# A spectral filter and a gated feed-forward block: the first batch in another order, and its weight rounding spread out

## The chip, the core and the metric

The kernel runs on one core of a Trainium2 chip. The metric is the device time of one execution in microseconds (us); lower is better. The kernel before takes 3011.8 us (median of three runs, 3008.76 to 3013.31).

The core has five engines that work side by side, each on its own list of instructions in order: TensorE (PE, with its weight loads listed apart as PEld), VectorE (DVE), ScalarE (ACT), GpSimd (POOL) and SyncE (SP), which here only issues transfers (DMA). They wait for each other with semaphores. Matmul results appear in PSUM, everything else is in SBUF; DRAM is reached by DMA.

## The reference

```python
# x: (8, 3008, 256) float32; filt_r, filt_i: (1505, 256)
X = np.fft.rfft(x, axis=1)
Y = X * (filt_r + 1j * filt_i)[None]
x = np.fft.irfft(Y, n=3008, axis=1).astype(np.float32).reshape(24064, 256)

g   = x @ w_gate                      # w_gate, w_val: (256, 1536), float64
val = x @ w_val
out = (g / (1 + np.exp(-g)) * val) @ w_out     # w_out: (1536, 256), float64
```

Eight batches of 3008 tokens go through a filter along the sequence, and each token then through a gated feed-forward block. The weights come in double precision; the kernel itself rounds them to single precision.

## The kernel before

**The filter.** A length of 3008 is 47 x 64. Stage 1 multiplies with a 47-point table, its result (D1) goes through DRAM (in the first batch it stays in SBUF and is turned with TensorE); stage 2 does the 64-point transform (`stage2a`), multiplies with the filter, and goes back (`stage2b`) in 12 pieces of two residues each; its result (D2) goes to DRAM; stage 3 multiplies with the inverse 47-point table and leaves y, one chunk of 752 tokens at a time. There are four chunks in a batch.

**The feed-forward block.** A chunk is worked on three times, once for each third ("group") of the 1536 hidden units, so a batch has 12 steps (chunk k, group g). Within a step a fast form of the matrix product needs combinations of weights and of tokens: P and Q products take y itself, A, B and E products take sums of two blocks of y (in `y_t`, made by `combine_sequence`) and combinations of weights (made by `combine_weights`). All 26 weight pairs of a group make 3.4 MB, which is kept in DRAM once made, and reloaded in four pieces for each step. The order within a step is a fixed list of tokens; W are the products with `w_out`, o their additions, S the sums of h, x.o the output stores, t the places where pieces of the filter of the following chunk or batch go:

```python
SCHEDULE = """
Q0 o3' t4.2' W2 f0 S00' S01' x0.o' t0.0 x1.o' Q1 t0.1 x2.o' P3 x3.o' f1 t4.3' W1 x4.o' S10' x03 S11'
s13 x5.o' P1 o1 t0.2 P0 o2 c1 D01 A13 g1 c0 ...            # a mark (') means: for the step before
"""
```

The function `pin` keeps each instruction where the program puts it.

**Rounding the weights.** There are 36 half blocks of 256 KB. One is rounded so (cut):

```python
def round_half(i):
    raw, (use, *at) = raws[i], weights[i][1]
    low, high = raw[:, :, :, 0], raw[:, :, :, 1]
    pw = rpool.tile(..., tag="pw", bufs=2)
    w = rpool.tile(..., tag="w", bufs=2)
    pin(v.tensor_scalar(out=man, in0=high, scalar1=0xFFFFF, op0=ALU.bitwise_and))         # L282
    pin(v.tensor_scalar(out=pw, in0=high, ... logical_shift_right, bitwise_and))           # L284
    pin(nc.scalar.activation(out=w, in_=man, func=AF.Copy, scale=2.0 ** -20, bias=1.0))    # L286
    pin(nc.scalar.activation(out=pf, in_=pw, func=AF.Relu, bias=off_t))                    # L288
    pin(nc.scalar.activation(out=pf, in_=pf, func=AF.Relu, bias=top_t, scale=-1.0))        # L289
    pin(nc.scalar.activation(out=pw, in_=pf, func=AF.Copy, scale=-(2.0 ** 23), ...))       # L290
    load_weights(i + NRAW - 1)
    yield
    pin(v.scalar_tensor_tensor(out=pw, in0=raw high, 0x80000000 ... and, or))              # L295
    pin(v.scalar_tensor_tensor(out=w, in0=raw low, scalar=2.0 ** -52, in1=w, mult, add))   # L298
    # then one to five products and sums on GpSimd, into wt_t, wt_1 or wo_t

def round_next():            # called at a token: starts one half and ends the one before
    ...
```

Some calls stand between the stages of the start, the others at fixed tokens of the first three steps:

```python
PREPARE = {(0, "B03"): [("k", 1, p) for p in range(4)], ...}     # "k": keep a group's weights in DRAM
for step, tokens in ((0, "Q0 P3 P0 Q2 A01 B01"), (1, "Q0 P3 P1 A13 P2 B13 Q3 A12 B02 B12"),
                     (2, "A13 P2 B01 A02")): ...                  # "r": round one half
```

**The start.** The order in which the first batch is read, and its stage 2:

```python
for i, n in enumerate((0, 2, 2, 4)):
    spec.load_x(i)                               # a quarter of x
    for _ in range(n):
        load_weights(len(raws))                  # a half block of weights
for i in range(3):
    spec.load_tables(i)                          # tables and filters of 4 of the 12 pieces
...
lag = 3
for u in range(N_TWO + lag):
    if u < N_TWO:
        spec.turn(u + 2); run(spec.stage2a(u)); spec.real_part(u + 3)
    if u >= lag:
        run(spec.stage2b(u - lag))               # ends with ACT's copy and the store of D2

def stage2a(self, u):                            # (cut)
    pin(v.tensor_tensor(out=pt, in0=ps, in1=fr, op=ALU.mult))     # fr: filter's real part on both
    pin(v.scalar_tensor_tensor(out=qt[lo], in0=ps[hi], ...))      # halves, copied by ACT (real_part)
    pin(v.tensor_tensor(out=qt[hi], in0=ps[lo], in1=fi, op=ALU.mult))
    pin(add(nc.gpsimd, pt, pt, qt))
```

Of the kernel before, what the change touches and what calls it, by code (L numbers as in the profile page):

```python
# [51 lines left out]
NJ = NM // 2  # L52
# [6 lines left out]
NH = 4  # L59
# [3 lines left out]
TOK = (0, 128, TH - 128)  # L63
NG = 3
# [35 lines left out]
PAIRS = ((0, 1), (1, 2), (2, 3), (0, 2), (1, 3), (0, 3))  # L100
ORDER = [t for t in SCHEDULE if t[0] in "PQABE"]
# [41 lines left out]
def kernel(  # L143
# [22 lines left out]
    xpool = pool("xp", 3)  # L166
# [24 lines left out]
    def weights_of(b, k, g):  # L191
        return wt_1 if (b, k, g) == (0, 0, 1) else wt_t

    dram_tiles = [wdpool.tile([2 * NS, N2, C], FP32, name=f"d{1 + i % 2}_{i // 2}")
                  for i in range(4)]
    w_dram = wdpool.tile([NG, 128, NPR, 2, 128], FP32, name="w_all")
# [34 lines left out]
    def weight_halves():  # L231
# [16 lines left out]
        for g in range(NG):  # L248
            for i in BLOCKS:
                yield from hid(g, i)  # L250
            for j in range(JB * (g - 1), JB * g) if g else ():
                yield from proj(j)
        for j in range(JB * (NG - 1), NJ):
            yield from proj(j)
# [3 lines left out]
    NRAW = 3  # L258
    N_EARLY = 16

    def load_weights(i):
# [6 lines left out]
        queue = nc.sync if i < 9 else nc.scalar  # L268
        pin(queue.dma_start(out=raws[i], in_=weights[i][0]))

    def round_half(i):
# [4 lines left out]
        pw = rpool.tile([128, 2, 128], U32, name=f"pw_{i}", tag="pw", bufs=2)  # L276
# [6 lines left out]
                            op0=ALU.bitwise_and))  # L283
        pin(v.tensor_scalar(out=pw, in0=high, scalar1=20, scalar2=0x7FF,  # L284
                            op0=ALU.logical_shift_right, op1=ALU.bitwise_and))
        pin(nc.scalar.activation(out=w, in_=man, func=AF.Copy, scale=2.0 ** -20, bias=1.0))  # L286
        pf = pw.bitcast(FP32)
        pin(nc.scalar.activation(out=pf, in_=pw, func=AF.Relu, bias=off_t))  # L288
        pin(nc.scalar.activation(out=pf, in_=pf, func=AF.Relu, bias=top_t, scale=-1.0))  # L289
        pin(nc.scalar.activation(out=pw, in_=pf, func=AF.Copy, scale=-(2.0 ** 23),  # L290
                                 bias=255 * 2.0 ** 23))

        load_weights(i + NRAW - 1)
# [3 lines left out]
                                   op0=ALU.bitwise_and, op1=ALU.bitwise_or))  # L297
        pin(v.scalar_tensor_tensor(out=w.rearrange(flat), in0=raw.rearrange(flat2)[:, :, 0],  # L298
                                   scalar=2.0 ** -52, in1=w.rearrange(flat),
                                   op0=ALU.mult, op1=ALU.add))  # L300
        e = nc.gpsimd
# [23 lines left out]
    halves = [round_half(i) for i in range(len(weights))]  # L325
    rounding = [0]

    def round_next():

        i = rounding[0]  # L330
        rounding[0] += 1
        for h in halves[i:i + 1] + (halves[i - 1:i] if i else []):
            next(h, None)

    def combine_weights(g, i, j):
# [5 lines left out]
        if d == 1:  # L341
            pin(negated_sum(m, ui, uj))
        else:
            pin(add(nc.vector, m, ui, uj))
            pin(nc.vector.tensor_scalar(out=m, in0=m, scalar1=-1.0 / d, scalar2=None, op0=ALU.mult))
# [8 lines left out]
    def reload_weights(g, piece):  # L354
        a, b = PIECES[piece]
        tc.keep_in_program_order(nc.sync.dma_start(out=wt_t[:, a:b], in_=w_dram[g, :, a:b]))

    PREPARE = {(0, "B03"): [("k", 1, p) for p in range(4)], (1, "B03"): [("k", 2, 0)],  # L360
               (2, "A01"): [("k", 2, p) for p in (1, 2, 3)]}
    for step, tokens in ((0, "Q0 P3 P0 Q2 A01 B01"), (1, "Q0 P3 P1 A13 P2 B13 Q3 A12 B02 B12"),
                         (2, "A13 P2 B01 A02")):
        for token in tokens.split():
            PREPARE.setdefault((step, token), []).append("r")
    for g, pairs in ((1, "0Q313 0A0201 0A1202 0B0212 0B1223 0A2303"),
                     (2, "1A0213 1E1201 1E0202 2Q112 2P123 2Q203")):
        for p in pairs.split():
            PREPARE.setdefault((int(p[0]), p[1:-2]), []).insert(0, ("c", g, int(p[-2]), int(p[-1])))
# [21 lines left out]
    class Spectral:  # L391
# [50 lines left out]
        def load_tables(self, i):  # L442

            n = NS // 3
# [6 lines left out]
        def load_t4(self, k, i):  # L451
            self.t4[k, i] = t4pool.tile([NK, NH, C], FP32, name=f"t4_{self.b}_{k}_{i}", tag="t4")
            self.load(out=self.t4[k, i], in_=self.d2_rows[:, ts(2 * k + i, NH), :])
# [486 lines left out]
```

## Time and profile before

| what | value |
|---|---|
| span of the profiled execution | 3008.6 us |
| TensorE, busy | 2930.9 us, 97% of the span |
| weight loads of TensorE, busy | 2836.1 us, 94% |
| VectorE, ScalarE, GpSimd, busy | 64%, 54%, 52% |
| data moved | 545.5 MB, 181 GB/s in the mean |

The profile is of one execution. Its page gives busy times of the engines, the span in 40 slices of 75 us (a digit is the busy share in tenths), the chain of work that ended last, and groups of equal instructions with their mean duration and with the idle time of the engine just before them and what ended it. In lines such as `wa<-y_t,wt_t` the output stands left, the inputs right; L626 is a line of the kernel (626 the products of a step, 703 the W products, 641 the ScalarE copy "f" that negates a first product, 219, 222 and 226 helpers for sums and differences, 548 stage 3, 505 stage 2a, 532 stage 2b). A timeline line gives the start, the duration, engine, line, operation and count of merged instructions, and in brackets the idle time before and what ended it. Matmuls are in float32[...], so one product of the program is several matmul instructions.

### The profile page before, as it was taken

How to read it: one execution, taken by the hardware profiler on the slowest of the kernel's cores; microseconds unless marked ns; L12 is line 12 of the kernel's file. 1: busy time of each engine (PE TensorE's matmuls, PEld its weight loads, DVE VectorE, ACT ScalarE, POOL GpSimd, SP SyncE). 2: the span in 40 equal slices, each digit the busy share in tenths (PEclk: the TensorE clock that was granted, in tenths of full speed). 3: DMA queues.
4: the chain of work that ended last, by engine and by line, in shares of the span. 5: the costliest groups of instructions: out<-in, count | busy, mean ns of one | idle time of the engine just before them, and what ended most of it. 6: DMA issues, size and time to landing. Idle time of an engine off the chain costs nothing.

```text
span 3008.6 us, 57532 instructions
## 1 busy us (share of the span) xinstructions
PE 2930.9 (97%) x20286; PEld 2836.1 (94%) x20286; DVE 1920.6 (64%) x4385; ACT 1627.2 (54%) x4206; POOL 1578.4 (52%) x1763
## 2 busy tenths in 40 slices
PE   7589999999999999999999999999999999999999
PEld 5479999999999999999999999999999999999999
DVE  5675676566765666557665576655676566766665
ACT  6565555555555555555555545555545555555554
POOL 3664645455645455546554556544655445654453
PEclk8789999999999999999999999999999999999999
DMA  8445665556655656456655575556664556544442
GB/s 218 138 169 184 214 199 165 185 186 194 212 165 179 207 188 213 150 186 207 198 174 184 173 227 184 182 171 194 197 215 156 188 186 202 193 161 145 139 135 90
DMA packets 203849, 545.53 MB, mean 181 GB/s; under 512 B 28992, under 2 KB 99760, under 8 KB 202704
## 3 DMA queue, kind: packets, MB, share of 16 engines
q1 hardware_dynamic: 153002, 466.50, 48.6%
q10 hardware_dynamic: 41632, 51.46, 5.2%
q0 software_dynamic: 8928, 23.89, 2.6%
q8 instruction: 163, 2.67, 0.4%
q14 instruction: 124, 1.02, 0.1%
HBM read 459.68 MB, written 82.05 MB: 180 GB/s over the span
## 4 chain that ended last, share of the span: by engine, by line
PE 92%; DVE 0%; ACT 0%; issue 0%; POOL 0%; ACTq 0%
PE wa L626 24%; PE wA L703 17%; PE wk L626 16%; PE we L626 12%; PE wG L703 8%; PE wF L703 4%; PE pd L548 3%; PE pa L465 3%; PE pb L505 2%; PE pc L532 2%; DVE o L219 0%; DVE pw L284 0%; DVE y L226 0%; DVE h L222 0%; DVE h L219 0%
## 5 line engine op out<-in xcount | busy, mean ns | idle before, releaser
L626 PE MATMUL wa<-y_t,wt_t 128*128 128x188 f32 x4560 | 900.1, 323 | 5.8 <-ACT m L661 2.7
L626 PEld LDWEIGHTS wa<-y_t,wt_t 128*128 128x128 f32 x4560 | 747.0, 190 | 31.2 <-issue 15.2
L626 PE MATMUL wk<-y,wt_t 128*128 128x188 f32 x3040 | 583.0, 325 | 34.2 <-ACT f L641 24.0
L219 POOL TENSOR_TENSOR h<-h 128x376 f32<-128x376 f32 x190 | 182.7, 984 | 815.9 <-DVE h L673 815.9
L703 PE MATMUL wA<-wo_t,h 128*128 128x128 f32 x4608 | 579.8, 276 | 3.7 <-DVE o L219 2.7
L703 PEld LDWEIGHTS wA<-wo_t,h 128*128 128x128 f32 x4608 | 565.1, 192 | 16.9 <-issue 12.0
L222 POOL TENSOR_TENSOR h<-h 128x376 f32<-128x376 f32 x570 | 553.0, 994 | 0.5
L626 PEld LDWEIGHTS wk<-y,wt_t 128*128 128x128 f32 x3040 | 491.9, 191 | 63.8 <-ACT f L641 25.4
L222 DVE TENSOR_TENSOR we<-we,m 128x376 f32<-128x376 f32 x576 | 319.0, 556 | 202.4 <-PE we L626 145.5
L626 PE MATMUL we<-y_t,wt_t 128*128 128x188 f32 x2280 | 440.5, 323 | 0.0
L626 PEld LDWEIGHTS we<-y_t,wt_t 128*128 128x128 f32 x2280 | 377.5, 190 | 0.1
L222 POOL TENSOR_TENSOR D<-f,f 128x376 f32<-128x376 f32 x288 | 280.2, 986 | 110.0 <-ACT f L641 109.3
L226 DVE SCALAR_TENSOR_TENSOR y<-wk,c 128x376 f32<-128x376 f32 x480 | 244.5, 543 | 141.0 <-ACT we L657 87.0
L661 ACT COPY m<-wa 128x376 f32<-128x376 f32 x576 | 272.2, 473 | 89.9 <-PE wa L626 88.8
L668 ACT ACTIVATE g<-wa 128x188 f32<-128x188 f32 x576 | 188.3, 327 | 196.1 <-PE wa L626 188.4
L703 PE MATMUL wG<-wo_t,h 128*128 128x128 f32 x2304 | 289.5, 276 | 0.6 <-DVE o L219 0.6
L703 PEld LDWEIGHTS wG<-wo_t,h 128*128 128x128 f32 x2304 | 282.7, 192 | 0.8 <-DVE o L219 0.8
L668 ACT ACTIVATE u<-we 128x188 f32<-128x188 f32 x576 | 189.3, 329 | 168.2 <-DVE we L222 149.2
L641 ACT ACTIVATE f<-wk 128x376 f32<-128x376 f32 x288 | 139.7, 485 | 242.2 <-PE wk L626 223.3
L645 ACT COPY c<-wk 128x376 f32<-128x376 f32 x288 | 136.1, 473 | 227.4 <-PE wk L626 227.2
L648 DVE SCALAR_TENSOR_TENSOR x<-wk,f 128x376 f32<-128x376 f32 x192 | 104.4, 544 | 236.8 <-PE wk L626 236.2
L657 ACT COPY we<-y 128x376 f32<-128x376 f32 x480 | 223.6, 487 | 31.3 <-DVE h L673 12.9
(128 smaller groups left out, 3856.3 us busy)
## 6 DMA issues: line engine op xcount, KB each, us to landing
wt_t<-w_all SPq DMA_DIRECT2D x186, 896.0 KB
wt_t<-w_all SPq DMA_DIRECT2D x186, 768.0 KB
t<-d SPq DMA_DIRECT2D x64, 384.0 KB
d<-t ACTq DMA_DIRECT2D x112, 192.0 KB
lent<-de_tbl SPq DMA_DIRECT2D x84, 256.0 KB
lent<-in_filt_r_dram SPq DMA_DIRECT2D x336, 64.0 KB
lent<-d SPq DMA_DIRECT2D x84, 256.0 KB
d<-lent ACTq DMA_DIRECT2D x84, 256.0 KB
```

Source lines behind the costliest of these rows:

```text
L219: return eng.tensor_tensor(out=dst, in0=a, in1=b, op=ALU.add)
L222: return eng.tensor_tensor(out=dst, in0=a, in1=b, op=ALU.subtract)
L226: return nc.vector.scalar_tensor_tensor(out=dst, in0=a, scalar=-1.0, in1=b, op0=ALU.mult, op1=ALU.subtract)
L465: pin(nc.tensor.matmul(out=ps[0:NK], lhsT=wf_t, rhs=self.x.pop(u), start=True, stop=True))
L626: pin(nc.tensor.matmul(out=ps[:, z], lhsT=self.wt[:, SLOT[p], z], rhs=rhs, start=start and z == 0, stop=True, skip_group_check=True))
L641: pin(act.mul(self.small(f"f{i}", f"f{i}", 1), t[f"k{i}"], -1.0))
L645: pin(act.copy(out=self.small(f"c{i}", f"c{i}", 1), in_=t[f"k{i}"]))
L648: pin(v.scalar_tensor_tensor(out=dst, in0=t[f"k{j}"], scalar=-1.0, in1=t[f"f{i}" if j == 3 else f"D{at}"], op0=ALU.mult, op1=ALU.add))
L657: pin(act.copy(out=self.bank(f"e{at}"), in_=t[f"y{at}"]))
L661: pin(act.copy(out=self.small(f"m{at}", "m", 4), in_=t[f"a{at}"]))
L668: pin(act.activation(out=self.small(op, "g", 3, 1)[:, 0], in_=ps[:, 1], func=AF.Silu))
L703: pin(nc.tensor.matmul(out=self.tiles[at][:, t, :], lhsT=self.hs[i][:, HID[p], t0:t0 + 128], rhs=wo_t[:, JB * q + i, WO[p], :], start=star ...
```

## The change

It concerns the first batch. Its steps ran (0,0) (0,1) (0,2) (1,0) and so on, in pairs of chunk and group, so all three groups' weights were needed within the first three steps. Now the first three chunks take turns: (0,0) (1,0) (2,0) (0,1) (1,1) (2,1) (0,2) (1,2) (2,2), then chunk 3. Group 1 is needed from step 3 on and group 2 from step 6, and weights are not reloaded until then. For this, y, its sums and the partial outputs of a chunk are kept in DRAM between its turns. The rounding of one half is cut into five pieces, of which one is issued at each of 24 evenly spaced places of a step. At the start, tables come in sixths, and in another order with x and weights; the copy of the filter's real part is left out for every third piece (which multiplies its two halves separately). D2 for chunk 0 is read in two row ranges into a table buffer. In all batches the input has two buffers instead of three, and the outputs two instead of one.

```diff
+NT = 3
+PAIRS_USED = ((1, 3), (0, 1), (0, 2), (1, 2), (2, 3), (0, 3))
-    xpool = pool("xp", 3)
+    xpool = pool("xp", 2)
-        return wt_1 if (b, k, g) == (0, 0, 1) else wt_t
+        return wt_1 if b == 0 and k < NT and g == 1 else wt_t
-    NRAW = 3
-    N_EARLY = 16
+    NRAW = 2
+    N_EARLY = 15
     ... round_half: pw in 3 buffers, and a yield after each of five pieces (cut)
-            pin(nc.vector.tensor_scalar(out=m, in0=m, scalar1=-1.0 / d, scalar2=None, op0=ALU.mult))
+            pin(nc.scalar.mul(m, m, -1.0 / d))
     ... PREPARE is replaced by (cut)
+    class Preparation:
+        def tick(self, step, n=1):
+            for _ in range(n):
+                if self.window and self.window[0] <= step:
+                    self.window = next(self.steps, None)
+        def finish(self, step): ...
+    TICKS = 24
     ... load_tables
-            n = NS // 3
+            n = NS // 6
     ... the start
-        for i, n in enumerate((0, 2, 2, 4)): ...
+        load = [("x", 0), ("x", 1), ("w", 0), ("x", 2), ("w", 1), ("x", 3), ("t", 0), ("w", 2),
+                ("t", 1), ("w", 3), ("t", 2), ("w", 4), ("w", 5), ("t", 3), ("w", 6), ("t", 4),
+                ("w", 7), ("t", 5)]
     ... after stage 1 of the first batch
+        for i in range(8, N_EARLY):
+            load_weights(i)
     ... in the loop over the 12 pieces
+                preparation.tick(0, 1 + u % 2)
+                spec.real_part(u + 1)
+                preparation.tick(0)
     ... before stage 3
+        preparation.tick(0, 14)
     ... the order of steps, what is kept and reloaded
+        if b == 0:
+            steps[:NT * NG] = [(k, g) for g in range(NG) for k in range(NT)]
+    for step in range(NT):
+        for d, token in ((2, "Q2"), (1, "A01"), (3, "Q3")):
+            chore(step, token, keep_sums, step, d)
+        chore(step, "Q2" if step == 0 else "W2", keep_y, step)
+    for step in range(NT - 1, NT * NG):
+        chore(step, "A02", lambda s: reload_y(order_of(0)[s + 1][0], s), step)
+    for step in range(NT, NT * NG):
+        chore(step, "Q3", lambda s: new_outs(0, *order_of(0)[s]), step)
     ... stage 3 of chunk k + 1 is done within step k, four pieces and one of stage 1 (before: over
     ... two steps or later), and in the list of tokens
+                if b == 0 and this and place * TICKS % len(SCHEDULE) < TICKS:
+                    preparation.tick(step)
-                if op in ends and not last and (b or step > 1):
+                if op in ends and not last and (b or step >= NT * NG - 1):
                     reload_weights((g + 1) % NG, ends[op])
```

## The prediction

> **What bounds the kernel now.** I read the page from the top: busy time in 40 slices first, because a share over the whole span hides a bad stretch. Then came the waits of TensorE, longest first, then the same engines in windows of 25 us, and last the timeline of TensorE from 80 to 260 us, to find where each step (a chunk with one group of blocks) begins. The busy rows of the page (one digit for each 75 us):
>
> ```profile
> PE   7589999999999999999999999999999999999999
> PEld 5479999999999999999999999999999999999999
> ...
> PEclk8789999999999999999999999999999999999999
> ```
>
> From the fourth slice on TensorE is full, its weight loads too, and its clock is granted in full. Only the first 225 us have anything to give. The waits of TensorE over the whole span (engine, line, what it waited for; total, times, longest) say the same, since all of them lie there:
>
> ```profile
> PE wk L626 <- ACT f L641: 28.8, 5, 19.8
> PE wpb L505 <- ACT room L495: 11.5, 1, 11.5
> PE wk L626 <- DVE y L219: 10.2, 1, 10.2
> PE wa L626 <- ACT m L661: 3.4, 2, 2.7
> ```
>
> The three largest wait for ScalarE or VectorE, none for a transfer. Windows of 25 us (busy us of PE, PEld, DVE, ACT, POOL, then granted clock, DMA share, GB/s):
>
> ```profile
> 0.00:25.00 25.00, 20.89 (x127) 17.02 (x128) 7.45 (x17) 10.09 (x16) 1.53 (x7) 0.95 0.95 247
> ...
> 100.00:125.00 25.00, 5.17 (x14) 3.76 (x14) 14.09 (x31) 14.41 (x33) 15.90 (x26) 0.57 0.28 80
> ...
> 300.00:325.00 25.00, 25.00 (x180) 24.69 (x179) 18.92 (x42) 12.19 (x32) 15.46 (x16) 1.00 0.70 222
> ```
>
> At 100 to 125 us the busiest engine, GpSimd, has work for 15.9 of 25 us, and DMA for a quarter. That is a chain of small dependent operations, not a full engine. Three lines of TensorE's timeline mark the beginnings of steps 0, 1 and 3; the second line shows the long wait inside step 0:
>
> ```profile
> 100.23 1.62 PE L626 MATMUL wk<-y,wt_t 128*128 128x188 f32 x4 [10.23 <-DVE y L219]
> ...
> 125.23 2.88 PE L626 MATMUL wk<-y,wt_t 128*128 128x188 f32 x8 [19.84 <-ACT f L641]
> ...
> 154.06 0.80 PE L626 MATMUL wk<-y,lent 128*128 128x188 f32 x4
> ...
> 240.61 0.80 PE L626 MATMUL wk<-y,wt_t 128*128 128x188 f32 x4
> ```
>
> Step 2 begins at 202.6 in the same list. So steps 0, 1, 2 take 53.8, 48.6 and 38.0 us; later ones take 29.9 us (the last "wk" of step 3 is at 255.6, of step 12 at 524.7: 269.2/9). From 240.6 to the end at 3008.6, **2768.0 us** are TensorE's own work, which the change leaves alone.
>
> What fills the first stretch is rounding the double-precision weights: 36 halves, each 4 operations on VectorE, 4 on ScalarE, then 1 to 5 on GpSimd. The groups of instructions between 100 and 230 us give their means:
>
> ```profile
> L284 DVE TENSOR_SCALAR pw<-raw 128x256 uint32<-128x256 uint32 x20 | 11.7, 585 | 0.0
> ...
> L282 DVE TENSOR_SCALAR w<-raw 128x256 uint32<-128x256 uint32 x20 | 11.1, 556 | 8.1 <-POOL lent L219 3.2 <-POOL wo_t L305 2.4 <-POOL wt_t L219 1.5
> ...
> L286 ACT ACTIVATE w<-w 128x256 f32<-128x256 uint32 x23 | 9.6, 417 | 23.0 <-DVE w L282 22.6 <-DVE w L298 0.4
> ```
>
> ScalarE waited 22.6 us for VectorE's first operation of a half, and that one waited for GpSimd to give back the buffer of two halves before. A half is recorded as one lump, so the three engines pass it round in about 3 us (L282 starts at 110.43, 113.43, 116.43 us), and the step's own work queues behind it.
>
> **What the Trainium skill says.** "Perfetto Trace Analysis", Optimization Strategy: where the most-contended engine changes over time, interleaving those regimes may help. That is what the change does, and the windows above show the two regimes. "SBUF — State Buffer", SBUF: two separate sides: VectorE in a two-port mode and GpSimd take a shared port pair as an exclusive lock, the loser blocks. The trace agrees as far as durations go: the L284 operations on the raw halves take 0.280 us at the least and 1.073 at the most for one shape. "TensorE: Matmul & The Clock Gate", What's actually happening: an idle window halves the clock. It was granted 0.50 from 110 to 125 us, and a "wk" product meanwhile averages 393 ns against 323 later. "DMA: Bandwidth & Descriptors", Queues, rings and completion order: descriptors of a ring are consumed in order; I use this below for writes queued behind loads, and no run has shown that yet.
>
> **The change part by part.**
>
> *Start, up to the first product (100.2 us before).* Ahead of the first tables stood four x loads and eight weight halves (5.2 MB) and a third of the tables (2.1 MB); now it is x (3.1 MB), two halves (0.5) and a sixth (1.05), 4.65 MB. At the 247 GB/s of the first window that is 19 us, some 21 with the landing. Stage 2 can start at about 24 us; its first matmul now starts at 35.6, and then stands from 38 to 50 behind four lumps of rounding (the 11.5 us wait). VectorE paces stage 2: three operations of 0.69 us for each of 12 pieces, 2.16 us each. The change leaves out ScalarE's copy of the filter for every third piece, which then has four operations: 8 x 3 + 4 x 4 = 40 at 0.71 is 28.4 us. Six halves are rounded in between (24 operations of 0.27 to 0.42 in VectorE's timeline before 50 us, 8.3 us): 37 us, so 24 + 37 = 61 against 75.5 for the last such operation before. One new wait works against it: seven more halves (1.8 MB) are loaded by SyncE's queue ahead of the first store of D2. 11.5 + 1.8 + 0.26 MB at 247 GB/s land at 55 us, and with four buffers the ScalarE copy of piece 4, due near 48, waits for it. I take 4 us of the 7 as lost: 65. From there to stage 3 took 10.8 us before (75.5 to 86.3) and its steps are the same: 76. Then y took 13.9 us with rounding in front; without most of it, 4 to 5. **First product at 80.**
>
> *Step 0.* Before, six halves stood in lumps in it and four more right ahead of it. Now 24 pieces of rounding (five make a half, so 4.8 halves) are spread over the tokens. TensorE's floor is low, as there is nothing yet to project: 29.9 less 84 matmuls of 0.112 (1.34 for 12) is 20.5. But stage 3 of the next chunk is now wholly in this step, sums on GpSimd come 5 us before the first A product, and chains are short of slack: **28 us**, to 108.
>
> *Steps 1 and 2.* They now need the same third of the weights as step 0, so no rounding is due before step 3. In step 1, GpSimd has 8 h sums and 3 differences at 0.99 (10.9 us), the next chunk's sums (three operations each of 128x376, 128x564 and 128x188, which take 0.99, 1.38 and 0.59 between 600 and 1320 us: 8.9) and 4.8 halves of some three operations at 0.46 (6.6): 26.4 of 29.9. VectorE has 19 of steady work (64% of 29.9) and 19 rounding operations at 0.51 (9.7): 28.8. Both fit, with little to spare, and each in fixed order: **33 us each**, to 174. Before, step 3 began at 240.6: 66.6 us less.
>
> *Steps 3 to 8.* They keep rounding (to step 6) and save and reload y, its sums and the outputs: in step 3 some 3.4 MB of weights stored, 2.5 of y and sums, 1.6 of outputs, 1.0 of x, 1.3 of halves, 1 of D1, near 11 MB in 30 us. 360 GB/s is above the 231 that the 25 us windows reach from 225 to 600 us (398 was seen in 5 us with weight stores). Weight reloads (20 MB) fall away in steps 2 to 7. I charge **6 us** for all six steps. Two input buffers instead of three in the other batches: x is issued about 12 us before its use instead of 18; I charge nothing.
>
> Sum: 80 + 28 + 33 + 33 + 6 + 2768 = 2948 span, and 3 for the measured median being above the profiled span (3011.8 and 3008.6): **2951 us**, a ratio of 0.980.
>
> **The rivals.** (1) *VectorE or GpSimd becomes the bound of steps 1 to 5*, as they come to 28.8 and 26.4 of 29.9 us. For it: the lock, and 4 halves with 6 combinations in step 2 before cost 8 us over 29.9. Against: those were lumps. It would make these steps 36 and the time about 2970. (2) *Reloads arrive late*: the next chunk's sums (1.7 MB in three loads) must land before its A products, behind stores in the same queue. The transfers total near the limit in steps 3 and 6; 3 us in each of six steps would make 2963. (3) *The start is bound by landing and not by VectorE*: then the gain there is 10 and not 20 us, 2961. (4) *Everything spread runs at TensorE's pace*: first product at 76, steps at 25, 30, 30 and no charge after: 161, a time of 2932. (5) *Two x buffers are too few*: 1 us at each of 112 pieces would return everything, about 3060. Against: in the steady part TensorE waits for no load at all, and DMA is busy 0.6.
>
> **Range and chances.** Rivals 1 to 3 pull up by 10 to 20 us, rival 4 down by 19, rival 5 is unlikely: 2930 to 2982. A gain of 2% means below 2951.6, which is my middle: 0.50 faster, 0.47 within 2%, 0.03 slower.
>
> **What would show it.** In the profile after: first "wk" near 80, steps 1, 2, 3 beginning near 108, 141, 174; no wait of TensorE for "f" over 5 us; TensorE full from about 110 us; a D2 copy of piece 4 ended by a DMA near 55. Wrong if idle time before A products is put down to DMA into the sums (rival 2), if "w" and "pw" operations on VectorE average above 0.7 us and TensorE waits for VectorE throughout steps 1 to 5 (rival 1), or if stage 1 in later batches waits for x (rival 5).

## The result, and the profile after

The changed kernel takes **3010.3 us** (median of 4 runs, 3006.7 to 3012.2), the kernel before, beside it on the same chip, 3012.6. The ratio is 0.9994, with a 95% interval of 0.9976 to 1.0011: no difference that can be told from none. The prediction was 2951 us, with 2930 to 2982 as its range. Of some 60 us that were to be gained, 2 arrived.

The profile (span 3004.9 us) was taken of the quickest of those runs. Single executions of this kernel differ by up to 5.5 us, so a span is good to some 3 us. The start of a step is no surer: from step 9 to the end all kernels below take 2587.1 to 2588.4 us, so what their spans differ in lies ahead of it. How long one step takes is surer: e13 and e15, which are alike up to step 3, agree within 0.2 us on each of steps 0 to 3, while their first products lie 1.5 us apart.

The page's busy rows, one digit for each 75 us (busy tenths of TensorE and of its weight loads, then its granted clock):

```profile
PE   7798999999999999999999999999999999999999
PEld 5787899999999999999999999999999999999999
...
PEclk9899999999999999999999999999999999999999
```

The second and third digits rose from 5 and 8 to 7 and 9: the first 225 us are fuller. But the fourth, a 9 before, is now an 8, and the fifth is just 9. In weight loads (4 7 9 9 before, 7 8 7 8 in the same places) it is plainer: the loss has moved from 75–225 us to 225–375. Windows of 25 us (busy us of PE, PEld, DVE, ACT, POOL, granted clock, DMA share, GB/s) show the same:

```profile
100.00:125.00 25.00, 18.71 (x92) 17.18 (x90) 16.89 (x39) 15.43 (x39) 11.87 (x20) 0.79 0.37 129
...
225.00:250.00 25.00, 19.88 (x107) 17.36 (x106) 13.71 (x37) 14.73 (x41) 5.00 (x11) 0.86 0.78 272
...
300.00:325.00 25.00, 20.52 (x126) 17.63 (x125) 17.59 (x45) 14.03 (x38) 9.45 (x13) 1.00 0.52 151
```

At 100 us TensorE went from 5.2 to 18.7 of 25 us, and its clock from 0.57 to 0.79. At 300 us it was full before and lacks 4.5 us now. At 225 us no engine is full, while DMA moves 272 GB/s at a share of 0.78 (before, 249 GB/s was the most in such a window between 75 and 425 us).

The longest waits of TensorE over the whole span (engine, line, what it waited for; total, times, longest):

```profile
PE wa L679 <- ACT wa L705: 8.5, 3, 5.1
PE wpc L571 <- DVE y_t L555: 7.5, 4, 2.8
PE wA L758 <- DVE o L224: 5.0, 6, 1.5
PE wpb L539 <- ACT room L529: 4.2, 2, 2.8
PE wk L679 <- ACT f L694: 4.1, 3, 2.3
```

The wait for f, 28.8 us before, is down to 4.1. In its place stand many waits of 1 to 5 us. TensorE's timeline gives the beginnings of steps 0, 1, 3 and 9:

```profile
93.90 1.62 PE L679 MATMUL wk<-y,wt_t 128*128 128x188 f32 x4 [1.52 <-DVE y L224]
...
133.36 0.80 PE L679 MATMUL wk<-y,wt_t 128*128 128x188 f32 x4
...
207.07 0.80 PE L679 MATMUL wk<-y,lent 128*128 128x188 f32 x4
...
416.86 0.80 PE L679 MATMUL wk<-y,wt_t 128*128 128x188 f32 x4
```

Step 3 begins 33.5 us sooner than before (240.6), step 9 only 4.6 us sooner (421.5). What the start brings is given back within six steps. From step 9 to the end nothing changed: 2588.0 us against 2587.1.

### The profile page after: what moved, and what is told of

It reads as the page before. It is cut to its first block, busy times and chain, and to the rows that moved or that the text cites. A ratio compares the mean times of both kernels' runs of the same rounds, so it can differ in the third digit from the quotient of the medians.

```text
span 3004.9 us, 57645 instructions
## 1 busy us (share of the span) xinstructions
PE 2938.8 (98%) x20286; PEld 2838.2 (94%) x20286; DVE 1939.4 (65%) x4380; ACT 1615.8 (54%) x4207; POOL 1583.5 (53%) x1763
## 4 chain that ended last, share of the span: by engine, by line
PE 89%; POOL 1%; DMA 1%; DVE 1%; ACT 1%; issue 0%; ACTq 0%; SPq 0%; DVEq 0%; POOLq 0%
PE wa L679 23%; PE wA L758 16%; PE wk L679 15%; PE we L679 12%; PE wG L758 8%; PE wF L758 4%; PE pd L587 3%; PE pa L499 3%; PE pc L571 2%; PE pb L539 2%; DMA raw<-in_moe_w_val_dram 0%; POOL h L227 0%; DVE o L224 0%; DMA lent<-in_filt_r_dram 0%; POOL wt_t L224 0%
## 5 line engine op out<-in xcount | busy, mean ns | idle before, releaser
L679 PE MATMUL wa<-y_t,wt_t 128*128 128x188 f32 x4464 | 884.2, 324 | 12.0 <-POOL wo_t L227 3.9
L679 PEld LDWEIGHTS wa<-y_t,wt_t 128*128 128x128 f32 x4464 | 733.6, 191 | 37.6 <-issue 18.4
L758 PEld LDWEIGHTS wA<-wo_t,h 128*128 128x128 f32 x4608 | 564.6, 192 | 22.2 <-issue 11.5
L679 PE MATMUL wk<-y,wt_t 128*128 128x188 f32 x2976 | 571.1, 325 | 4.2 <-ACT f L694 2.7
L679 PEld LDWEIGHTS wk<-y,wt_t 128*128 128x128 f32 x2976 | 482.0, 191 | 29.8 <-issue 19.8
L679 PE MATMUL we<-y_t,wt_t 128*128 128x188 f32 x2232 | 432.4, 323 | 0.0
L679 PEld LDWEIGHTS we<-y_t,wt_t 128*128 128x128 f32 x2232 | 370.5, 190 | 0.0
## 6 DMA issues: line engine op xcount, KB each, us to landing
t<-d SPq DMA_DIRECT2D x62, 384.0 KB
```

The source lines that it names most:

```text
L679: pin(nc.tensor.matmul(out=ps[:, z], lhsT=self.wt[:, SLOT[p], z], rhs=rhs, start=start and z == 0, stop=True, skip_group_check=True))
L758: pin(nc.tensor.matmul(out=self.tiles[at][:, t, :], lhsT=self.hs[i][:, HID[p], t0:t0 + 128], rhs=wo_t[:, JB * q + i, WO[p], :], start=star ...
```

## The experiments

Step starts of all kernels, from the same view (us; step 0 is the first "wk"), with the span of the profile; each kernel was profiled once:

| kernel | step 0 | 1 | 2 | 3 | 7 | 9 | span |
|---|---|---|---|---|---|---|---|
| before | 100.2 | 154.1 | 202.6 | 240.6 | 360.9 | 421.5 | 3008.6 |
| changed | 93.9 | 133.4 | 169.4 | 207.1 | 354.8 | 416.9 | 3004.9 |
| e1 third raw buffer | 94.3 | 133.8 | 167.3 | 205.4 | 342.2 | 409.1 | 2997.3 |
| e2 rounding inside stage 2 | 86.1 | 123.5 | 160.3 | 198.6 | 345.8 | 411.7 | 2999.8 |
| e3 combinations spread | 94.4 | 132.2 | 168.0 | 205.1 | 349.0 | 413.0 | 3001.3 |
| e4 no rounding of groups 1, 2 | 96.6 | 137.8 | 168.7 | 199.1 | 318.9 | 382.9 | 2970.8 |
| e5 = e1 + e2 + e3 | 87.9 | 125.4 | 160.5 | 198.3 | 332.5 | 399.9 | 2988.0 |
| e6 = e1 without GpSimd's part | 95.2 | 138.9 | 174.8 | 207.7 | 333.6 | 399.7 | 2987.9 |
| e7 = e1 without VectorE's and ScalarE's part | 94.9 | 130.2 | 161.1 | 195.8 | 323.2 | 386.8 | 2975.0 |
| e8 = e5, ScalarE's operations sooner | 89.2 | 130.6 | 166.0 | 204.2 | 343.8 | 406.7 | 2994.7 |
| e9 = e5, one ScalarE operation to a piece | 87.8 | 125.6 | 159.2 | 197.3 | 327.7 | 390.3 | 2978.3 |
| e10 = e5, pieces three tokens sooner | 88.0 | 123.2 | 160.6 | 197.3 | 335.2 | 400.3 | 2988.3 |
| e11 = e5 without ScalarE's part | 88.0 | 124.1 | 155.7 | 192.9 | 321.0 | 386.3 | 2974.4 |
| e12 = e5, rounding in lumps | 87.9 | 129.3 | 174.6 | 217.4 | 376.6 | 441.7 | 3029.8 |
| e13 = e9, start of step 0 clear | 85.9 | 116.2 | 152.6 | 189.6 | 320.1 | 385.3 | 2973.5 |
| e14 = changed, one ScalarE operation to a piece | 93.0 | 131.6 | 167.5 | 205.8 | 350.6 | 416.0 | 3004.1 |
| e15 = e13, y reloaded sooner | 84.4 | 114.8 | 151.2 | 188.4 | 318.9 | 384.0 | 2972.2 |

In every kernel the rounding is over before step 7 begins. Steps 7 and 8 together take 60.6 us before, 62.1 in the changed kernel and 62.6 to 67.5 in the others: in ten of these a load of y lands late in step 8 (e15). So what an edit does to the rounding is read from the start of step 7, and a span can hide part of it.

### Late raw halves (e1)

What does the traffic at 225 us do to the step? The waits of VectorE from 200 to 350 us in the changed kernel:

```profile
DVE wa L701 <- POOL D L227: 6.7, 2, 3.4
...
DVE w L285 <- DMA raw<-in_moe_w_out_dram: 5.5, 1, 5.5
DVE w L285 <- DMA raw<-in_moe_w_val_dram: 5.0, 2, 4.5
```

The chain of waits from 226 to 345 us (start, us, what) names the same loads; here are its two longest pieces:

```profile
231.40 9.13 DMA raw<-in_moe_w_val_dram
...
251.91 5.21 DMA raw<-in_moe_w_val_dram
```

Each lands 5 to 9 us after its issue, while the stores of the group's weights, the outputs and the sums are under way. With two buffers it is issued only three pieces of rounding before VectorE wants it (4.7 us in the first case). VectorE works in fixed order, so the step's own operations stand behind.

```
-    NRAW = 2
+    NRAW = 3
...
+        elif i % 3 == 2:
+            raws[i] = lent[:, 13 * NV * C:] ...     # 2 KB of `lent` that wt_1 does not use
```

> A third buffer for the raw halves (in a spare piece of `lent`), so that each load is issued one half sooner. In the changed kernel the last wk of step 3 starts at 227.0 us and that of step 9 at 431.8: 204.8 us for six steps that would take 181 at 30.2 each. Theory 'late raws' (with two buffers a half is loaded only some 4 us before VectorE wants it, and lands 5 to 9 us after issue): the 12.4 us of VectorE waiting for raw between 200 and 400 us fall below 2, these six steps take 190 to 195, and the span falls by 10 to 14 us. Rival 'full engines' (VectorE and GpSimd are too full there anyway): the waits for raw go, others take their place, and the span falls by less than 4.

Measured: the waits for raw between 117 and 327 us are gone, and the span fell by 7.6 us to 2997.3 (one timed run: 2999.1). Steps 3 to 7 took 168.0 us instead of 178.8 (373.4 − 205.4 and 385.9 − 207.1), and step 7 began 12.6 us sooner: the 10 to 14 expected of the span. But step 8 took 35.7 instead of 31.0, so that the six steps came to 203.7 and not to 190 to 195; e15 comes back to that. The theory holds; what it leaves over is larger than what it takes away.

### The lock at the start (e2)

VectorE's groups of instructions in stage 2 of the changed kernel (26 to 79 us; shapes, count, busy us, mean ns, idle before):

```profile
L289 DVE TENSOR_SCALAR pw<-wt_t 128x256 uint32<-128x256 uint32 x6 | 8.2, 1362 | 0.0
L304 DVE SCALAR_TENSOR_TENSOR w<-wt_t,w 128x256 f32<-128x256 uint32 x7 | 7.7, 1105 | 0.0
```

These operations take 0.29 and 0.42 us when nothing is in their way. Here they are recorded right behind the third VectorE operation of a piece, at which GpSimd begins its add (1.37 us, from 31.76): L289 begins at 31.92 and ends at 33.28, just after the add.

```
-                run(spec.stage2a(u))
+                piece = spec.stage2a(u)
+                next(piece), next(piece)
                 preparation.tick(0, 1 + u % 2)
+                run(piece)
```

> The one or two pieces of rounding that follow a piece of stage 2 are recorded before its third VectorE operation instead of after it, so that they no longer lie beside GpSimd's add of that piece (1.27 us). Theory 'lock' (VectorE's operations on SBUF alone, beside a GpSimd operation, are held up until it ends): the L289 and L304 groups of the start fall from 1.36 and 1.5 us to about 0.3 and 0.45, a piece of stage 2 from 4.1 to about 3.1 us, and the first product comes at about 84 instead of 93.9 us; the span falls by 7 to 10. Rival 'latency' (the pace of stage 2 is set by ScalarE's copies and the hand-over, and VectorE only fills the time): the durations fall, but the first product moves by less than 3 us.

Measured: the same two groups in this kernel (26 to 74 us):

```profile
L304 DVE SCALAR_TENSOR_TENSOR w<-wt_t,w 128x256 f32<-128x256 uint32 x7 | 3.0, 425 | 0.2
L289 DVE TENSOR_SCALAR pw<-wt_t 128x256 uint32<-128x256 uint32 x6 | 1.8, 294 | 0.2
```

A piece took 3.5 us (from 29.35 to 71.74 us for 12) instead of 4.1, and the first product came at 86.1, 7.8 us sooner. Step 7 began 9.0 us sooner; the span fell by 5.1, as step 8 took 34.8 instead of 31.0. The work is the same and only its place differs: the first L289, for one, now begins at 32.53, 0.05 us ahead of the add, and takes 0.29. So the place beside the add is what stretched these operations. "SBUF — State Buffer", section "SBUF: two separate sides", of the Trainium skill says that whoever holds the shared port pair keeps it for the whole instruction and the other one fully blocks; an L289 that ends 0.15 us after the add fits that.

### Combinations on end (e3)

```
-                for pair in PAIRS_USED:
-                    yield window
-                    combine_weights(at[0], *pair)
+                pairs = [(at[0], *pair) for pair in PAIRS_USED]   # groups 1, 2:
...
+                if n in (0, 3) and pairs:                         # two to each later half
+                    combine_weights(*pairs.pop(0))
```

> The six weight combinations of groups 1 and 2 (two GpSimd operations of 0.7 to 0.9 us each) are no longer done at six pieces of rounding on end but two to a half, between the pieces of the next three halves. Theory 'burst' (twelve such operations on end hold up GpSimd's D and h operations from 282 to 300 us, in step 5): the step from the last wk of step 5 to that of step 6 falls from 38.2 us to 32 to 34, and the one of group 1 (step 2 to 3, 40.8) by some 3; the span falls by 5 to 9. Rival 'late raws set the pace': under 2 us, since these steps still wait for raw halves.

GpSimd's timeline in the changed kernel, in step 5:

```profile
288.71 0.73 POOL L227 TENSOR_TENSOR wt_t<-wt_t 128x256 f32<-128x256 f32 x1
289.40 0.91 POOL L224 TENSOR_TENSOR wt_t<-wt_t 128x256 f32<-128x256 f32 x1
290.27 2.13 POOL L227 TENSOR_TENSOR h<-h 128x376 f32<-128x376 f32 x2
...
299.38 1.91 POOL L227 TENSOR_TENSOR D<-f,f 128x376 f32<-128x376 f32 x2
```

From 282 us on it is never idle, and the D that VectorE and then TensorE need comes last. Measured: from the last wk of step 5 to that of step 6 it is now 32.4 us (301.3 to 333.7) instead of 38.2, as expected; group 1's stretch hardly changed (39.9 against 40.8). Step 7 began 5.8 us sooner, within the 5 to 9 expected of the span, although VectorE's waits for raw halves in 200 to 350 us are still 12.7 us (11.0 in the changed kernel). The span fell by 3.6, since step 7 then took 32.9 us instead of 31.1: its chain goes back to a load of sums of y that landed 12.2 us after its issue. So the burst was real.

### What turn-taking costs without rounding (e4)

Leaves out the loading and rounding of the weights of groups 1 and 2; all stores and reloads stay.

```
-        for i in range(len(weights)):
+        for i in range(4 * JB + 2 * JB):       # the halves of group 0 only
+    # wt_1 and the rest of wo_t: 17 memsets to 0.01 on GpSimd in steps 0 and 1
```

> Leaves out the loading and rounding of the weights of groups 1 and 2 (their room is filled with a constant by 17 memsets on GpSimd in steps 0 and 1; all transfers of y, sums, outputs and weights stay). What is left after step 0 is the order of steps with its stores and reloads. If rounding in its present form is what costs time (theories 'late raws', 'burst', 'full engines'): steps 1 and 2 take 30 to 31 us each, the six steps from the last wk of step 3 to that of step 9 take 181 to 186 instead of 204.8, and the span is 25 to 32 us shorter than the changed kernel's. If the stores and reloads of turn-taking cost time by themselves (theory 'traffic'): these six steps still take over 195.

TensorE's timeline of this kernel, steps 3 and 9:

```profile
199.08 0.80 PE L679 MATMUL wk<-y,lent 128*128 128x188 f32 x4
...
382.93 0.80 PE L679 MATMUL wk<-y,wt_t 128*128 128x188 f32 x4
```

Six steps in 183.8 us, 2.9 more than before the change (180.9); steps 1 and 2 in 30.9 and 30.4. The span is 34.1 us shorter than the changed kernel's. The stores and reloads by themselves, with no half loaded beside them, are all but free; rounding costs over 30 us even when it is spread. The theory "traffic" falls.

### Three losses, or one (e5)

The edits of e1, e2 and e3 together.

> The three edits together: third raw buffer, rounding inside the pieces of stage 2, weight combinations spread. Alone their profiled spans were 7.6, 5.1 and 3.6 us under the changed kernel's 3004.9. Theory 'three separate losses': they add, span about 2988.6, a ratio of 0.993 to the kernel before. Rival 'one loss seen from three sides' (the same hold-up in steps 3 to 6, which any of them relieves): span 2993 to 2996.

Measured: span 2988.0, median 2987.1 (2983.9 to 2989.8), ratio to the kernel before 0.9913 (0.9896 to 0.9929). The spans add up, 16.9 us against 16.3 for the sum, but this is partly luck. The changed kernel's profile is of its quickest execution and e5's of its slowest (by the medians e5 is 23.2 us under), and the late load of y in step 8 takes 3.8 to 4.7 us from e1 and e2 alike, and from e5 only once. Up to the start of step 7 the edits alone bring 12.6, 9.0 and 5.8 us, and together 22.3, some four fifths of their sum. So the losses overlap somewhat; that they are one loss (2993 to 2996) is ruled out. Steps 1 to 5 still take 31 to 38 us each.

### Which engine (e6, e7, e11)

Three kernels leave out parts of the rounding of groups 1 and 2. e6 and e7 stand on e1, e11 on e5.

```
e6:  GpSimd's operations of a half and the combinations left out
     17 memsets on GpSimd in steps 0 and 1, as in e4
e7:  four VectorE and four ScalarE operations of a half left out, GpSimd multiplies a constant
     (pw of group 0 in two buffers instead of three)
e11: the four ScalarE operations of a half left out
```

> On the kernel with the third raw buffer (span 2997.3): leaves out GpSimd's operations of the rounding of groups 1 and 2, with the weight combinations; loads and the operations on VectorE and ScalarE stay. Without any of the rounding the span was 2970.8, so 26.5 us are to be shared out. Theory 'GpSimd is the full engine': the span falls to 2980 or less. Theory 'hand-over' (a rounding operation in VectorE's or ScalarE's fixed order holds up the step's own operation behind it): the span stays above 2988.

> The counterpart: on the kernel with the third raw buffer, leaves out the operations of VectorE and ScalarE of the rounding of groups 1 and 2 (GpSimd multiplies a constant instead, all its operations and the weight combinations stay, and so do the loads). Theory 'hand-over': the span falls to 2980 or less, steps take 30 to 32 us. Theory 'GpSimd is the full engine': it stays above 2988.

> The three edits together (span 2988.0), leaving out the four ScalarE operations of each half of groups 1 and 2; VectorE's four, GpSimd's, the weight combinations and the loads stay. Theory 'ScalarE and its hand-over is the cost of the vector part': the span falls by 8 to 15. Theory 'VectorE itself is the cost (it is busy 169 of 222 us in this stretch)': the span falls by less than 4.

Measured: without GpSimd's part 9.4 us less (2997.3 to 2987.9), without VectorE's and ScalarE's 22.3 less (to 2975.0), of 26.5 for both. Without ScalarE's part alone, on e5, 13.6 less (2988.0 to 2974.4). The steps share it out more evenly. From the start of step 1 to that of step 7 e1 takes 208.4 us, e6 194.7, e7 193.0, and e4, which leaves out both parts, 181.1. So GpSimd's part costs 13.7 us there, VectorE's and ScalarE's 15.4, both 27.4. What else parts the spans of e6 and e7 lies outside: step 0 takes 43.7 us in e6 (39.5 in e1), where four memsets of 0.85 us stand in GpSimd's order, and 35.3 in e7; step 8 takes 35.0 and 31.5. So neither theory holds alone: "GpSimd is the full engine" asked for 2980 or less in e6, and "hand-over" on VectorE and ScalarE leaves half of the cost unexplained. e11 puts 10.2 us of these steps (207.1 to 196.9) on ScalarE's operations and what hangs on them. Over the stretch as a whole none of the engines is full. From 108 to 330 us (222 us), e7 and then e1:

```profile
108.00:330.00 222.00, 212.57 (x1397) 200.24 (x1396) 134.47 (x308) 119.18 (x311) 143.53 (x198) 0.97 0.72 236
```

```profile
108.00:330.00 222.00, 198.19 (x1265) 180.94 (x1265) 166.09 (x375) 143.50 (x383) 144.52 (x190) 0.97 0.65 215
```

VectorE goes from 134 to 166 busy us, ScalarE from 119 to 144. At 75% and 65% (GpSimd 65%) they have room in the sum, and TensorE still is busy 14 us less in the same stretch. Step 2 is the exception: GpSimd is busy 29.6 of its 38.0 us in e1, about as long as TensorE needs for a step (30.2), and e6 takes 32.9 there. "Perfetto Trace Analysis", Identifying the Most-Contended Engine, takes the occupancy of these engines as the way to the bottleneck. Over this stretch it would name VectorE, the highest of the three; but GpSimd's operations cost about as much (e6), so a share alone does not size the loss. Which operation stands in front of which counts too, as the next runs show.

### How the pieces are cut (e8, e9, e12, e14)

VectorE's waits from 108 to 330 us in e5 begin with one that belongs to the rounding itself: its pw operation of one piece needs ScalarE's last operation of the piece before, which stands behind ScalarE's own work for the step.

```profile
DVE pw L303 <- ACT pw L300: 12.8, 10, 3.1
DVE y L231 <- ACT we L719: 9.4, 9, 1.8
DVE h L735 <- ACT u L730: 5.1, 7, 1.6
```

e8 moved ScalarE's two operations of the third piece into the second, which then had three:

```
+        pin(nc.scalar.activation(out=pf, in_=pf, func=AF.Relu, bias=top_t, scale=-1.0))
+        pin(nc.scalar.activation(out=pw, in_=pf, func=AF.Copy, ...))
         load_weights(i + NRAW - 1)
         yield
-        (the same two operations)
```

> The three edits together, and the two ScalarE operations of a half's third piece moved into its second, so that VectorE's first combination (L300) comes a whole piece (1.25 us) after ScalarE's last operation that it needs. In the kernel with the third raw buffer VectorE waited 11.9 us between 117 and 327 us in these places. Theory 'hand-over': the waits fall under 4 us and the span by 3 to 8 us more than the three edits give. Rival 'VectorE is merely full': the waits go but others come, under 2 us.

Measured: 6.7 us longer by span, median 2994.1, ratio 0.9941 (0.9926 to 0.9956). Step 7 even begins 11.3 us later than in e5; step 8 then took 31.2 instead of 34.8 us, since y came in time. The waits for pw fell as meant, but others came, and they are those of the step's own chain (same view, e8):

```profile
DVE h L735 <- ACT u L730: 8.8, 7, 2.8
DVE y L231 <- ACT we L719: 7.8, 7, 2.1
DVE h L735 <- ACT g L730: 7.0, 9, 1.7
DVE pw L303 <- ACT pw L298: 5.7, 5, 1.6
```

The waits for u and g rose from 8.9 to 15.8 us in sum: three rounding operations on end (some 1.5 us) hold up the Silu that a step waits for. My expectation was wrong in its sign, and the run says what to do instead. e9 gives each piece at most one operation of ScalarE and one of VectorE:

```
         pin(... Relu, bias=top_t ...)
+        yield
+        pin(v.scalar_tensor_tensor(out=w ...))
         pin(... Copy, scale=-(2.0 ** 23) ...)
         yield
         pin(v.scalar_tensor_tensor(out=pw ...))
         yield
-        pin(v.scalar_tensor_tensor(out=w ...))
-        yield
```

> The three edits together (span 2988.0), and the operations of a half dealt out so that no piece holds two of ScalarE: third piece ScalarE's second Relu alone, fourth VectorE's w and ScalarE's Copy, fifth VectorE's pw. The run before put three ScalarE operations into one piece and was 6.7 us slower, though its waits of VectorE for ScalarE fell from 12.8 to 5.7 us. Theory 'bunches on ScalarE' (a step's own copy or Silu stands behind the bunch): the span falls by 3 to 7 us under 2988.0. Rival 'VectorE's waits for pw': no change or up, as its pw operation follows ScalarE's Copy no later than before.

Measured: span 2978.3, 9.7 us under e5, median 2979.2 (2978.9 to 2980.1), ratio 0.9890 (0.9875 to 0.9905). Step 7 begins 4.8 us sooner, within the 3 to 7 expected; most of the rest came in step 8 (31.0 us against 34.8), whose load of y was in time here. Leaving ScalarE's operations out (e11) brings 11.5 us up to step 7, so dealing them out brings under half of that.

e12 goes the other way: all five pieces of a half at one place, every fifth place.

```
-                    preparation.tick(step)
+                    due[0] += 1
+                    if due[0] % 5 == 0:
+                        preparation.tick(step, 5)
```

> The three edits together (span 2988.0), with the five pieces of a half recorded at one place, every fifth place, as the kernel before did; orders, loads and buffers stay. If spreading is worth what the change meant: steps 1 to 6 are longer by 2 to 4 us each and the span is 10 to 20 us longer. If a lump costs no more than five pieces apart: within 3 us.

Measured: 41.8 us longer by span, median 3031.9, ratio to the kernel before 1.0064 (1.0047 to 1.0081), slower than both. Same view, e12:

```profile
DVE pw L303 <- ACT pw L300: 46.0, 24, 4.3
```

But these are not the lumps of the kernel before. There a place starts one half and ends the one before, and the 24 such VectorE operations between 100 and 240 us waited for ScalarE not at all; here a half is handed from VectorE to ScalarE and back at one place, and VectorE waited 1.9 us for each. So the run shows what it costs to keep a hand-over inside one place, and not what spreading is worth against the old lumps: that stays open.

e14 is e9's edit on the changed kernel, with none of the others.

> The changed kernel with this one edit alone: no piece holds two of ScalarE's operations (two raw buffers, rounding behind the pieces of stage 2 and combinations on end as in the changed kernel, span 3004.9). On top of the three edits it brought 9.7 us. Theory 'hand-over is a loss of its own': 6 to 10 us, span 2995 to 2999. Rival 'it shows only where the loads of raw halves are in time': 3 us or less.

Measured: median 3002.8, ratio 0.9966 (0.9953 to 0.9979), against 0.9994 (0.9976 to 1.0011) for the changed kernel; the spans, 3004.1 and 3004.9, and the starts of step 9, 416.0 and 416.9, hardly differ. By the medians the edit brings some 7 us, by the spans 1 (the slowest of its five executions against the quickest of four). The start of step 7 sides with neither: it comes 4.2 us sooner (350.6 against 354.8), nearly the 4.8 of e9, and step 8 then takes 34.2 us instead of 31.0, with the load of y in its chain. The wait for pw falls from 15.4 to 4.2 us (88 to 400 us), while the waits for raw halves stay (12.4 and 12.5). So the edit has some 4 us of its own in these profiles, between what the two theories said.

### Places (e10)

```
-                if ... place * TICKS % len(SCHEDULE) < TICKS:
+                if ... (place + 3) * TICKS % len(SCHEDULE) < TICKS:
```

> The three edits together (span 2988.0), with the pieces of steps set three tokens earlier in the order of a step (same number, same spacing). It measures how much hangs on the exact places. If pieces cost by their number and length alone: within 2 us. If the cost is that of single operations which happen to stand ahead of one on the chain: 3 us or more, either way.

Measured: span 2988.3, median 2989.8, ratio 0.9924 (0.9910 to 0.9939), which is within 0.3 us (span) of e5; but step 7 begins 2.8 us later, and the median is 2.7 us higher. That lies between the two expectations: the places matter by some 3 us in the sum, and single steps moved either way (step 0 took 35.2 instead of 37.4 us, step 4 34.5 instead of 31.4).

### Step 0 (e13)

In all kernels with the change so far step 0 took 35 to 44 us. e13 keeps rounding out of it until the first two VectorE operations of the chain have been recorded.

```
+                a = 23 if step == 0 else 0
+                n = len(SCHEDULE) - a
-                if ... place * TICKS % len(SCHEDULE) < TICKS:
+                if ... place >= a and (place - a) * TICKS % n < TICKS:
```

> The kernel with one ScalarE operation to a piece (span 2978.3), and no piece of rounding in step 0 ahead of its first two VectorE operations of the chain (x03, s13); the 24 pieces of that step follow on the rest of it, a little closer. There TensorE stood 5.4 us before the first A product: VectorE's s13 came after a rounding operation that itself waited 1.7 us for GpSimd, which had the sums of y to do. Theory 'rounding in front of the chain in step 0': that wait falls under 2 us and the first A product comes at about 94 instead of 98.3 us; span 3 to 5 us shorter. Rival 'the sums of y on GpSimd set it' (they end at 95.4): the wait stays, span within 1 us.

TensorE's timeline at its first A product, in e9 and then in e13:

```profile
98.31 1.59 PE L688 MATMUL wa<-y_t,wt_t 128*128 128x188 f32 x4 [5.37 <-POOL wo_t L227]
```

```profile
91.78 0.88 PE L688 MATMUL wa<-y_t,wt_t 128*128 128x188 f32 x4 [1.43 <-DVE wa L710]
```

The wait is 1.4 us, and step 0 takes 30.3 us instead of 37.7. Step 1 begins 9.4 us sooner than in e9 (2.0 of them from ahead of step 0), step 7 still 7.6 sooner, and step 9 5.0 (step 8 waits for y again). Median **2975.6** (2975.3 to 2976.1), ratio **0.9874** (0.9857 to 0.9890): the quickest full kernel of this study, 1.3% under the kernel before.

### The reload of y (e15)

In e1, e2, e4, e5, e6 and e10 to e14 the chain in step 8 goes back to a load of y that stood in SyncE's queue behind table loads and landed 8.0 to 9.3 us after its issue. Step 8 takes 32.5 to 35.7 us in these, and 31.0 to 31.5 in the changed kernel, e3, e7, e8 and e9, where no such load is in the chain. The two loads in e13's chain (start, us, what):

```profile
361.38 5.94 DMA lent<-de_tbl
...
369.49 8.07 DMA y<-y
```

```
-        chore(step, "A02", lambda s: reload_y(...), step)
+        chore(step, "A02" if step < 4 else "P3", lambda s: reload_y(...), step)
```

> The kernel with the clear start (median 2975.6, span 2973.5), with the reload of the next chunk's y from step 4 on recorded after P3 and not after A02, so half a step sooner and ahead of the filter loads of the next batch in SyncE's queue. In step 8 of that kernel TensorE's chain goes back to a load of y that was issued at 369.5 us, behind a load of the tables that waited for its buffer, and landed 8.1 us later. Theory 'reloads arrive late' (rival 2 of the prediction): step 8 falls from 32.5 us to 30.5 or less, TensorE's chain there holds no DMA of y, span 2 to 4 us shorter. Rival 'the load finds the same full queues earlier': within 1 us.

Measured: median 2976.2, ratio 0.9880 (0.9863 to 0.9896), no different from e13. Step 8 fell from 32.5 to 31.0 us and y left its chain, but step 7 rose from 32.7 to 34.0, with the table and D1 loads of the next batch in its chain. The queue passes the delay on to the next in line.

## Why the prediction was wrong, point by point

The predicted beginning of step 9 follows from its own sum: 174 + 180.9 + 6 = 360.9. It came at 416.9. The 56 us are:

| term | predicted | measured | short |
|---|---|---|---|
| first product | 80 | 93.9 | 13.9 |
| step 0 | 28 | 39.5 | 11.5 |
| steps 1 and 2 | 66 | 73.7 | 7.7 |
| steps 3 to 8 (180.9 and the charge of 6) | 186.9 | 209.8 | 22.9 |

What failed is the step from the sums to the time: rounding was taken to cost little or nothing as long as each engine's sum stayed under the length of a step. Steps 3 to 6 were charged nothing for it, and it cost 26 us (e4); in stage 2 its operations were put at 8.3 us and took 20.0; steps 1 and 2, into which it was to fit, took 73.7 us and not 66.

- **Start.** VectorE's first operation of stage 2 came at 28.8 and not 24 us (4.8 us), its last at 77.7 and not 65 (7.9 more), and from there to the first product it was 16.2 instead of 15. The term that failed is the rounding inside stage 2: 24 operations at 0.27 to 0.42 us, 8.3 in all; the 22 that came between 28.8 and 77.7 us took 20.0. They were sized from operations with no GpSimd add beside them; L289 took 1.36 us. The prediction quoted the lock and the 0.280 to 1.073 us, and then used the low end. e2 gets 7.8 us back. The charge of 4 us for D2's store was wrong too, and hid 4 us of this: ScalarE's copy of piece 4 waited for no DMA.
- **Step 0.** The 28 us took TensorE's floor at full clock, but the granted clock there was 0.74 on average (93.9 to 133.4 us). (The 393 ns that the prediction gives for a product at half clock are its mean from 100 to 230 us; from 110 to 125 none ran.) And the first A product waited 3.9 us and another one 2.3. e13 shows rounding ahead of the chain as the cause of most of it: 30.3 us without, against 37.7 in e9, with a granted clock of 0.94 against 0.86.
- **Steps 1 and 2** "both fit" by the sums of the prediction (VectorE 28.8 and GpSimd 26.4 of 29.9 us, in step 1), and took 36.0 and 37.7. The sums were near: VectorE was busy 26.0 and 26.7 us, GpSimd 25.9 and 29.2. What was wrong is the conclusion from them. A fixed order lets one operation that is not ready hold up all behind it: e9 takes 33.7 us for step 1 and e5 35.2, with the same operations dealt out otherwise. In step 2, where GpSimd's sum alone is near a whole step, that did not help (38.1 against 37.7).
- **Steps 3 to 8** carry the largest error, and it is one of omission. The 6 us were charged for stores and reloads, and e4 measures 2.9 for them: that was no more than charged. Nothing was charged for the rounding that goes on in steps 3 to 6: 26 us (209.8 − 183.8). The cut from three raw buffers to two was not charged at all; e1 sizes it at 11 us in steps 3 to 7.
- **Rest.** The steps after step 9 were as predicted, within 1 us, and two buffers for x cost nothing visible: rival 5 fell.
- **Rivals.** Rival 1 came true in its size: steps 1 to 5 took 37.6 us on average (36 foreseen), and its sum of 2970 was still too low because it stopped at step 5 and left the start as it was. Its own test failed, though: the means of "w" and "pw" operations are 0.44 to 0.64 us in these steps, under 0.7, and neither engine is full over them, GpSimd in step 2 excepted. The runs show that the order of the pieces is part of what bound the steps (e8, e9, e11), and that GpSimd's part costs nearly as much as the other two engines' (e6, e7); the lock's share in these steps no run separates. Rival 2 did not show in the changed kernel, where no TensorE wait names a DMA into the sums; it shows at 1 to 5 us in step 8 of ten of the kernels above, and in step 7 of e3 and e13 (loads of sums). Rival 3 fell: stage 2 began 4.8 us late, and TensorE's last wait ahead of it (0.9 us) was for ScalarE's copy of stage 1's result, no transfer.
- **Signs.** No wait for f over 5 us: right. Full from about 110 us: wrong, full only from about 400.

Not settled: by what way GpSimd's part costs its 13.7 us, and what VectorE's own operations have in the 15.4: the lock, the order, or in step 2 GpSimd's sum. No run separated these in the steps.

## What to carry to other kernels

Background work in fixed-order queues is not sized by the busy sum: cut it so that each piece puts at most one short operation in front of each engine's next own one, and keep whole pieces between operations that hand over from one engine to another. When a change spreads work over more steps, charge every step it now passes through, and check that its loads are issued earlier than they take to land in the busiest of these steps. A first sign that gains are given back later is the start of each step in the timeline, not the busy share of the span; and when edits are compared, read them where the part they touch ends, before an unrelated wait adds its own 4 us.

## What the runs showed of the hardware that I had not expected

- A VectorE operation of 0.29 us beside a GpSimd add of 1.37 us took 1.36 us, in all six cases (1.359 to 1.366); the operation before it, begun 0.05 to 0.12 us ahead of the add, took its usual 0.29.
- A 256 KB load took up to 9.1 us from its issue in step 3, where DMA moved 272 GB/s in a window of 25 us.
- Three ScalarE operations on end, some 1.5 us, put the start of step 7 11.3 us later than one and two (e8 against e5); one at a time put it 4.8 us sooner (e9).
